# Another order of pools, conversions and evictions in a fused attention, gated MLP and mixture kernel

## The chip, the cores and the metric

One core of a Trainium2 chip runs the whole program. The time is device microseconds of one execution; where several runs are given, their median. The profile shows one further execution, taken by the hardware profiler.

## The reference

Three layers follow each other. Attention with a mask by clusters (2 batches, 8 heads, 768 positions, 64 features), a gated MLP on its 1536 tokens of 512 features, and a mixture of four experts:

```python
sims = einsum(q / |q|, centroids / |centroids|)          # the same for k; argmax over 16 clusters
scores = where(q_assign == k_assign, q @ k.T / 8, -1e9)
x = softmax(scores) @ v                                  # to 1536 x 512
x = (sigmoid(x @ w_gate) * (x @ w_val)) @ w_out          # 512 -> 1536 -> 512
p = domain_probs / (domain_probs.sum(-1) + 1e-9)
out = sum over e of p[:, e] * (relu(x @ w1[e]) @ w2[e])  # 4 experts, 512 -> 1024 -> 512
```

The weights of the MLP come as float64, everything else as float32.

## The kernel before, in words

Every fp32 product is made of three matmuls on parts of 128 x 128 by 384 or 512 columns: an operand is split into a high part (fp32r, by ScalarE, ACT) and a low part (the rest, by VectorE, DVE, or GpSimd, POOL). Within a `manual_schedule` block each engine works through its instructions in the order in which the program text issues them, so an instruction that waits holds up all that stands behind it on its engine.

**Attention.** 96 items (batch, head pair, half, 128 queries): PE makes scores S (L432), DVE their negated maximum nm (L435), ACT the exponentials (L443), PE transposes them (L452), ACT and DVE split the transposed block into ph (L455) and pl (L456), and PE multiplies with v (L465, L466). The tables SLOT, FIRST, START, EARLY, SOON and TAIL say behind which item, and where in it, each piece of other work is issued; in TAIL the items are counted from the last. `xadd` (L507) and `xscale` (L510) scale the result of a head pair and write it to X; `right_operands` makes of X the sums t1 to t4 (L525) and the operands h, l (ACT L534, DVE or POOL L537) for the MLP.

**Conversion of weights.** A float64 weight lies as two 32-bit words. "mag": ACT takes the magnitude of the high word (L653) and scales the low word (L655). "bits": DVE clips (L660), shifts (L661) and puts the sign back (L662). "round": POOL adds the low word (L667). The result is in tiles cv (w_gate, w_val) or co (w_out). Then w_gate and w_val get four sums sf (L697) and are split into w1h (ACT L705) and w1l (POOL L706); w_out is split into woh (ACT L763) and wol (POOL L764).

**Layer 1, the gated MLP** (`moe1`). The 1536 hidden features are cut into six slices p of 256, the tokens into two batches b. `gate(p, b)` and `value(p, b)` each are one `seven`: seven products of six matmuls (L788) in four PSUM banks ph, with DVE's combinations (L801 to L823) between them; the evictions of gate are ACT's sigmoid (L860), those of value DVE's product sg (L872) and its split into G (ACT L873, POOL L874). `outp(p, b)` multiplies G with w_out (48 matmuls, L672 to L674, banks po) and adds to acc (ACT L893 in p = 0, DVE L895 after). The order in the loop is gate(p,0), outp(p-1,1), value(p,0), gate(p,1), outp(p,0), value(p,1). Each call takes a list of work, issued piece by piece between its products or evictions: conversions of the next weights stand there. `outp` with `soon=True` takes four banks and first makes the f = 0 half of all four, otherwise it ends one bank after the other.

**Mixture layer** (`moe2`). 32 pairs (b, e, g); `hidden(i)` is again a `seven`, evicted by ACT as h2h (L1060) and by DVE as h2l (L1061); `outp(i)` multiplies with w2 (L1084 to L1086), DVE adds into the result (L1091). `conv_in2` makes a pair's w1h and w1l, `conv_out2` its wo parts (ACT L1040, POOL L1041) from r2, which `load_out2` (L1022) fetches into a pool of one buffer; `operands` makes the seven right operands of a batch (sums POOL L1009, splits ACT L1005, DVE or POOL L1006). The beginning of this layer's work is issued within the last calls of layer 1.

The memory of `pools` is handed on: a tile of a later pool waits until the last reader of what lay there before is done.

Of the kernel before, what the change touches and what calls it, by code (L numbers as in the profile page):

```python
# [5 lines left out]
F32 = mybir.dt.float32  # L6
# [22 lines left out]
def r2(ap):  # L29
# [50 lines left out]
class Net:  # L80
# [460 lines left out]
    def attention(self):  # L541
# [9 lines left out]
        for key in START:  # L551
            if key[0] == "W":
                self.warm(int(key[2:]))
            else:
                begin.pop(key)()
        for n in range(NP):
            steps = [(k, go) for k, go in begin.items() if k[0] == str(n)] if n < 2 else \
                [("%d %s" % (n, name), go) for name, go in self.prep(n)]
            for key, go in steps + [("%d %s" % (n, name), go) for name, go in self.finish(n)]:
                if key in FIRST:  # L560
                    at, pos = FIRST[key]
                else:
                    at, pos = SLOT[key[2:]]
                    at += n * PER
# [3 lines left out]
        def pair(o):  # L568
            pool, tags = (self.nat0, ("nk", "nq")) if o == 5 else (self.op if o in (1, 2, 6) else self.xp, ("h%d" % o, "l%d" % o))
# [6 lines left out]
        pool = self.nc.gpsimd  # L576
# [12 lines left out]
        for k in range(2):  # L589
# [8 lines left out]
                "t1": self.late[0]["t1"],  # L598
# [243 lines left out]
    def moe1(self, xadd, xscale):  # L842
# [35 lines left out]
        def outp(p, b, work=(), soon=False):  # L878
# [53 lines left out]
        for p in range(1, NP):  # L932
# [5 lines left out]
        gate(0, 0, [[lambda: split0(6, Q), vs[0]], [lambda: split0(2, V), vs[1]], [vs[2]] + d[0], d[1] + [vs[3]],  # L938
                    d[2], d[3] + d[4] + [o0["split"]], [xadd, xscale]])
# [8 lines left out]
        for p in range(1, NP):  # L948
# [24 lines left out]
        outp(NP - 1, 0, [[lambda: cin[0](Q)], [], [], [cin[1]], [cin[2]], [cin[3]], [cin[4]], [out[0]]])
# [6 lines left out]
        ys, ysplit = self.operands(0, [room(self.op, t, F32) for t in ("h1", "l1", "h2", "l2")])  # L980
# [5 lines left out]
        self.first_in = []  # L986
# [60 lines left out]
    def moe2(self):  # L1047
# [54 lines left out]
        late = self.first_in  # L1102
# [20 lines left out]
    def run(self):  # L1123
# [13 lines left out]
        with ExitStack() as a:  # L1137
# [72 lines left out]
```

## Time and profile before

| | |
|---|---|
| median of 3 runs | 1098.1 us (1096.81 to 1098.77) |
| the profiled execution | 1095.45 us, of which 1093.7 us are the span |
| mean granted clock of PE | 0.986 |
| busy, PE / DVE / POOL / ACT | 1043.5 / 821.6 / 638.9 / 549.1 us |
| chain that ended last | PE 69%, POOL 11%, DVE 8%, issue 6%, DMA 3%, ACT 2% |
| attention | until about 280 us |
| layer 1 | until about 595 us |
| mixture layer | from about 590 us to the end |

The times count from the start of the span. A busy share is a mean over stages: in the last half PE does not pause, in the first half it does. The granted clock is a fraction of PE's full rate; 0.5 is the lower of its two levels (1.2 of 2.4 GHz). In the waits, "engine line <- other line" puts an idle time of the first engine down to the instruction that released it; in the timeline the bracket behind a row is the idle time before it.

### The profile page before, as it was taken

The page shows a single profiled execution, that of the slowest core. Times are in us where ns is not written, and L with a number is a line of the kernel's source. Part 1 is how long each engine was busy: PE and PEld are TensorE (multiplying, and loading weights), DVE is VectorE, ACT ScalarE, POOL GpSimd, SP SyncE. Part 2 cuts the span into 40 slices and gives each one's busy share as a digit, 9 for nine tenths or more (in the row PEclk, how much of TensorE's full clock was granted, in tenths as well). Part 3 has the DMA queues.
Part 4 walks back from the last instruction along what each step waited for, and adds up shares of the span by engine and source line. Part 5 has one row for each costly group of instructions (what it writes and reads, how often), then busy time and mean ns, then how long its engine had stood idle before and what let it go on. Part 6 is the DMA issues. An engine that isn't in the chain of part 4 may idle for free.

```text
span 1093.7 us, 16218 instructions
## 1 busy us (share of the span) xinstructions
PE 1043.5 (95%) x5813; PEld 971.4 (89%) x5813; DVE 821.6 (75%) x1408; ACT 549.1 (50%) x1155; POOL 638.9 (58%) x567
## 2 busy tenths in 40 slices
PE   6989999998898999898999999999999999999998
PEld 6889999987698999898998999899988998999887
DVE  6979999998666676666659877776678867766765
ACT  4879999887565444444434433343334433333320
POOL 6547778776567666666778544444445644444430
PEclk8999999999999999999999999999999999999999
DMA  8677767753111111222110312221222222211201
GB/s 174 135 187 175 173 155 165 159 147 94 56 39 58 59 58 58 77 63 73 58 59 19 113 43 78 77 77 39 77 77 97 81 74 77 78 57 60 78 20 58
DMA packets 86480, 95.86 MB, mean 88 GB/s; under 512 B 42720, under 2 KB 59456, under 8 KB 86400
## 3 DMA queue, kind: packets, MB, share of 16 engines
q1 hardware_dynamic: 86256, 94.80, 31.7%
q8 instruction: 46, 0.75, 0.3%
q14 instruction: 34, 0.28, 0.1%
q10 hardware_dynamic: 144, 0.03, 0.0%
HBM read 65.07 MB, written 3.19 MB: 62 GB/s over the span
## 4 chain that ended last, share of the span: by engine, by line
PE 69%; POOL 11%; DVE 8%; issue 6%; DMA 3%; ACT 2%; SPq 0%; POOLq 0%; DVEq 0%; ACTq 0%
PE ph L788 27%; PE po L1085 8%; PE po L1086 8%; PE po L1084 8%; PE T L452 4%; PE S L432 4%; POOL w1l L706 2%; PE PV L465 2%; PE PV L466 2%; PE po L673 2%; PE po L674 1%; PE po L672 1%; DMA rwo<-in_moe_w_out_dram 1%; DMA L<-hiq 1%; POOL sf L697 1%
## 5 line engine op out<-in xcount | busy, mean ns | idle before, releaser
L1041 POOL TENSOR_TENSOR wol<-r,woh 128x512 fp32r<-128x512 f32 x62 | 80.2, 1294 | 156.9 <-ACT woh L1040 156.6
L1091 DVE SCALAR_TENSOR_TENSOR acc<-po,pn,acc 128x512 f32<-128x512 f32 (+1 forms) x181 | 129.7, 742 | 36.3 <-PE po L1086 36.3
L1086 PE MATMUL po<-woh,h2l 128*128 128x512 f32 (+1 forms) x374 | 145.7, 390 | 0.0
L1085 PE MATMUL po<-wol,h2h 128*128 128x512 f32 (+1 forms) x374 | 145.6, 389 | 0.0
L1084 PE MATMUL po<-woh,h2h 128*128 128x512 f32 (+1 forms) x374 | 145.1, 388 | 0.0
L706 POOL TENSOR_TENSOR w1l<-sf,w1h 128x512 fp32r<-128x512 f32 x88 | 115.0, 1328 | 42.7 <-ACT w1h L705 42.7
L1060 ACT ACTIVATE h2h<-ph 128x384 fp32r<-128x384 f32 x128 | 62.7, 490 | 122.4 <-PE ph L788 96.1
L788 PE MATMUL ph<-h,w1h 128*128 128x384 f32 x336 | 114.4, 341 | 5.6 <-DVE u L801 2.6
L788 PE MATMUL ph<-l,w1h 128*128 128x384 f32 x336 | 113.1, 337 | 0.9 <-POOL l L537 0.7
L788 PE MATMUL ph<-h,w1l 128*128 128x384 f32 x336 | 113.1, 337 | 0.0
L456 DVE TENSOR_TENSOR pl<-T,ph 128x384 fp32r<-128x384 f32 x192 | 97.1, 547 | 19.2 <-ACT ph L455 17.8
L705 ACT ACTIVATE w1h<-sf 128x512 fp32r<-128x512 f32 x88 | 55.4, 632 | 82.7 <-DVE sf L697 68.1
L1061 DVE SCALAR_TENSOR_TENSOR h2l<-ph,h2h 128x384 fp32r<-128x384 f32 x128 | 70.9, 554 | 34.0 <-ACT h2h L1060 30.8
L455 ACT ACTIVATE ph<-T 128x384 fp32r<-128x384 f32 x192 | 84.5, 492 | 18.0 <-PE T L452 16.9
L435 DVE TENSOR_REDUCE nm<-S 128x1 f32<-128x768 f32 x96 | 90.9, 947 | 2.0 <-PE S L432 1.1
L432 PE MATMUL S<-R,L 80*128 80x384 f32 (+1 forms) x384 | 92.1, 362 | 0.2
L452 PE MATMUL T<-ident,P 128*128 128x128 f32 x576 | 83.3, 278 | 9.4 <-DVE pl L456 8.4
L706 POOL TENSOR_TENSOR w1l<-r,w1h 128x512 fp32r<-128x512 f32 x64 | 68.6, 1074 | 38.1 <-ACT w1h L705 38.1
L443 ACT ACTIVATE P<-S,nm 128x768 f32<-128x768 f32 x96 | 87.5, 912 | 2.5 <-DVE nm L435 2.1
L452 PEld LDWEIGHTS T<-ident,P 128*128 128x128 f32 x576 | 67.7, 142 | 17.5 <-DVE pl L456 12.0
L1086 PEld LDWEIGHTS po<-woh,h2l 128*128 128x128 f32 x374 | 70.2, 188 | 14.5
L1085 PEld LDWEIGHTS po<-wol,h2h 128*128 128x128 f32 x374 | 70.2, 188 | 13.9
(276 smaller groups left out, 2860.2 us busy)
## 6 DMA issues: line engine op xcount, KB each, us to landing
r<-in_moe_w_dram SPq DMA_DIRECT2D x64, 512.0 KB, 4.5
L<-hiq SPq DMA_DIRECT2D x32, 192.0 KB, 4.8
R<-hik SPq DMA_DIRECT2D x32, 192.0 KB, 4.9
raw<-in_moe_w_val_dram SPq DMA_DIRECT2D x12, 512.0 KB, 3.8
rwo<-in_moe_w_out_dram SPq DMA_DIRECT2D x11, 512.0 KB, 3.5
raw<-in_moe_w_gate_dram SPq DMA_DIRECT2D x10, 512.0 KB, 3.6
nq<-in_q_dram SPq DMA_DIRECT2D x16, 192.0 KB, 3.8
nk<-in_k_dram SPq DMA_DIRECT2D x16, 192.0 KB, 4.4
```

Of the source, the lines that this page charges most:

```text
L432: nc.tensor.matmul(ps[:, a, 0:384], l[0:k, c], r[0:k, a * 384:a * 384 + 384], start=l is L1, stop=l is L2)
L435: nc.vector.tensor_reduce(nm, ps[:, :, 0:384], axis=AX.XY, op=ALU.max, negate=True)
L443: nc.scalar.activation(r2(pt), ps[:, :, 0:384], AF.Exp, bias=nm, scale=1.0, accum_out=P["sums"][:, i:i + 1])
L452: nc.tensor.transpose(ps[:, j, :], pt[:, c:c + 128], self.ident)
L455: nc.scalar.activation(hi, ps, AF.Copy)
L456: nc.vector.tensor_tensor(lo, ps, hi.bitcast(F32), op=ALU.subtract)
L706: nc.gpsimd.tensor_tensor(lo[:, sl], x, hi[:, sl].bitcast(F32), op=ALU.subtract)
L788: nc.tensor.matmul(ps, x[:, a, j], y[:, j], start=first and j == 0 and k == 0, stop=j == 1 and k == 2, skip_group_check=not first)
L1084: nc.tensor.matmul(ps, Hh[:, f, c], wh[:, dc], start=f == 0, stop=False)
L1085: nc.tensor.matmul(ps, Hh[:, f, c], wl[:, dc], start=False, stop=False)
L1086: nc.tensor.matmul(ps, Hl[:, f, c], wh[:, dc], start=False, stop=f == 1)
L1091: nc.vector.scalar_tensor_tensor(a, ps, pe, a, op0=ALU.mult, op1=ALU.add)
```

## The change

It has six parts.

1. *Pools* (`run`). In the attention the pools stand in the order pp, sm, ac, up, vvp, qk, ptp (qk was first). Behind it tmp, wom and a new pool opx (operands h1, l1, h2, l2, h6, l6) come ahead of co, sg and op; these six operands lay in op before.
2. *TAIL*. The three bits of each w_val half are issued in one item, the rounding right behind them in the same item; xadd and xscale of the last head pair but one come behind the second rounding, t1 at the third item from the end.
3. *SOON*. The loads, magnitudes, bits and roundings of w_gate and the first part of w_out stand at other, mostly later items; a load is further ahead of its magnitude.
4. *gate(0, 0)*. The split of o0 is issued behind the first product, the steps of o1's conversion one place later each.
5. *The loop*. The conversion e of o1 moves from value(p, 0) to gate(p, 1); its split comes behind the fifth product. outp(p, 0) has `soon=True`. In outp(0, 0) and outp(5, 1) the first half starts with two of the three matmuls of all four banks.
6. *The end of layer 1*. The sums of conv_in2(1) go from DVE to POOL; conv_out2(0) and load_out2(1) go to the end of outp(5, 1).

```diff
 TAIL = {
     "open": (-12, 0), "load10": (-12, 0), "load11": (-12, 0), "sums0": (-12, 2), "outer1": (-11, 2),
-    "split00": (-11, 2), "split01": (-11, 2), "split02": (-10, 2), "split03": (-10, 2), "t1": (-10, 2),
-    "mag10": (-9, 2), "bits10": (-8, -8, -7), "round10": (-7, 2), "mag11": (-7, 2), "bits11": (-6, -6, -5),
-    "round11": (-5, 2), "sums1": (-3, 2), "table": (-3, 2),
+    "split00": (-11, 2), "split01": (-11, 2), "split02": (-10, 2), "split03": (-10, 2),
+    "mag10": (-9, 2), "bits10": (-8, -8, -8), "round10": (-8, 1), "mag11": (-7, 2), "bits11": (-6, -6, -6),
+    "round11": (-6, 1), "xadd6": (-5, 0), "xscale6": (-5, 0), "sums1": (-5, 2), "t1": (-3, 2), "table": (-3, 2),
 }
...
-            def part(ps, d, c, f):
+            def part(ps, d, c, f, some=range(3)):
                 dc = slice(d * 128, d * 128 + 128)
                 t = self.outers[2 * p + f]
-                self.mm3(ps, t["hi"][:, dc], t["lo"][:, dc], Gh[:, f, c], Gl[:, f, c], f == 0, f == 1)
+                for k in some:
+                    x, y = (("hi", Gh), ("lo", Gh), ("hi", Gl))[k]
+                    nc.tensor.matmul(ps, t[x][:, dc], y[:, f, c], start=f == 0 and k == 0, stop=f == 1 and k == 2)
...
                 if soon:
                     banks = [bank() for _ in range(4)]
-                    for d in range(4):
-                        part(banks[d], d, c, 0)
+                    for some in ((0, 1), (2,)) if n == 0 and (p == 0 or b == 1) else (range(3),):
+                        for d in range(4):
+                            part(banks[d], d, c, 0, some)
...
-        gate(0, 0, [[lambda: split0(6, Q), vs[0]], [lambda: split0(2, V), vs[1]], [vs[2]] + d[0], d[1] + [vs[3]],
-                    d[2], d[3] + d[4] + [o0["split"]], [xadd, xscale]])
+        split0(6, Q)
+        split0(2, V)
+        gate(0, 0, [[vs[0], o0["split"]], [vs[1]] + d[0], [vs[2]] + d[1], [vs[3]] + d[2], d[3] + d[4], [], [xadd, xscale]])
...
+            value(p, 0, [[], [o0["split"]]])
             e = conv(o1)
-            value(p, 0, [[], [o0["split"]], [], e[0], e[1], e[2], e[3] + e[4]])
             if p + 1 < NP:
                 c, d, split = conv(g, 0), conv(g, 1), g["split"]
-                gate(p, 1, [[o1["split"]], c[0], c[1], c[2], c[3], c[4]])
+                gate(p, 1, [e[0], e[1], e[2], e[3] + e[4], [o1["split"]] + c[0], c[1] + c[2], c[3] + c[4]])
                 outers[2 * p + 2]["load"]()
-                outp(p, 0, [d[0], d[1], d[2], d[3] + d[4], total(g), [split[0]], [], [split[1]]])
+                outp(p, 0, [d[0], d[1], d[2], d[3] + d[4], total(g), [split[0]], [], [split[1]]], soon=True)
                 value(p, 1, [load(U[p + 1][1]), [split[2]], [split[3]]])
-        gate(NP - 1, 1, [[o1["split"]]])
+        gate(NP - 1, 1, [e[0], e[1], e[2], e[3] + e[4], [o1["split"]]])
         self.load_out2(0)
...
-        outp(NP - 1, 0, [[lambda: cin[0](Q)], [], [], [cin[1]], [cin[2]], [cin[3]], [cin[4]], [out[0]]])
+        outp(NP - 1, 0, [[lambda: cin[0](Q)], [], [], [cin[1]], [cin[2]], [cin[3]], [cin[4]], []])
...
-        value(NP - 1, 1, [[ys[0], out[1], lambda: self.load_out2(1)], [lambda: ysplit(0, V), ys[1]], [ys[2]], [], [], [],
-                          [cin[0], lambda: ysplit(4, V)]])
-        outp(NP - 1, 1, [[ys[3], lambda: ysplit(5, V)], [cin[1]], [lambda: ysplit(3, V)], [cin[2]],
-                         [lambda: ysplit(1, V)], [cin[3]], [lambda: ysplit(6, Q)], [lambda: ysplit(2, V), cin[4]]], soon=True)
+        value(NP - 1, 1, [[ys[0]], [lambda: ysplit(0, V), ys[1]], [ys[2]], [ys[3]], [], [], [lambda: ysplit(4, V)]])
+        outp(NP - 1, 1, [[lambda: ysplit(5, V), lambda: cin[0](Q)], [], [lambda: ysplit(3, V)], [cin[1]],
+                         [lambda: ysplit(1, V)], [cin[2]], [lambda: ysplit(6, Q), cin[3]],
+                         [lambda: ysplit(2, V), cin[4], out[0], out[1], lambda: self.load_out2(1)]], soon=True)
```

Of SOON one line, then the pools:

```diff
-    "load00": (12, 2), "load01": (13, 2), "abs00": (15, 2), "low00": (24, 2), "bits00": (24, 25, 27), "round00": (28, 2),
+    "load01": (13, 2), "load00": (14, 2), "abs01": (24, 2), "bits01": (25, 27, 36), "low01": (27, 2), "round01": (37, 2),
...
-            self.qk = self.pool(a, "qk", 3)
             self.pp = self.pool(a, "pp", 3)
             self.sm = self.pool(a, "sm", 2)
             self.ac = self.pool(a, "ac", 1)
+            self.up = self.pool(a, "up", 2)
             self.vvp = self.pool(a, "vvp", 2)
+            self.qk = self.pool(a, "qk", 3)
             self.ptp = self.pool(a, "ptp", 2)
-            self.up = self.pool(a, "up", 2)
...
-        self.tmp = self.pool(es, "tmp")
...
+            self.tmp = self.pool(m, "tmp")
+            self.wom = self.pool(m, "wom", 2)
+            self.opx = self.pool(m, "opx")
             self.co = self.pool(m, "co")
-            self.wom = self.pool(m, "wom", 2)
             self.sg = self.pool(m, "sg")
             self.op = self.pool(m, "op")
```

In the changed kernel the lines of the MLP carry numbers that are 4 higher up to outp, 6 or 7 higher behind it.

The change on POOL in the attention's tail, first before (tB is t1, the second and the last row with cv are the roundings of w_val, A and R are xadd and xscale, sf the sums):

```order
L525 TENSOR_TENSOR tB<-R_62 128x768
L667 TENSOR_TENSOR cv<-cv,raw 128x512
L507 TENSOR_TENSOR A<-A,W 128x768
L510 TENSOR_TENSOR R_62<-A,rb 128x768
L667 TENSOR_TENSOR cv<-cv,raw 128x512
L697 TENSOR_TENSOR sf<-cv 128x256
```

and now:

```order
L671 TENSOR_TENSOR cv<-cv,raw 128x512 x2
L507 TENSOR_TENSOR A<-A,W 128x768
L510 TENSOR_TENSOR R_62<-A,rb 128x768
L701 TENSOR_TENSOR sf<-cv 128x256
L701 TENSOR_TENSOR sf<-sf,cv 128x256
L701 TENSOR_TENSOR sf<-cv 128x256
L701 TENSOR_TENSOR sf<-cv,sf 128x256
L525 TENSOR_TENSOR tB<-R_62 128x768
```

The second rounding has moved ahead of xadd and xscale, beside the first, and tB from the front to the end, behind the sums.

DVE from value(3, 0) into gate(3, 1), before (u, ph and sg are the products' combinations and the gating; co is the conversion of o1, cv that of the next w_gate):

```order
L872 TENSOR_TENSOR sg<-sg,ph_5700 128x384
L872 TENSOR_TENSOR sg<-sg,ph_5680 128x384
L660 TENSOR_SCALAR co<-co 128x512
L818 TENSOR_TENSOR ph_5732<-u_5679,ph_5732 128x384
L661 TENSOR_SCALAR co<-co 128x512
L823 TENSOR_TENSOR ph_5708<-u_5678,ph_5708 128x384
L872 TENSOR_TENSOR sg<-sg,ph_5732 128x384
L872 TENSOR_TENSOR sg<-sg,ph_5708 128x384
L662 SCALAR_TENSOR_TENSOR co<-rwo,co 128x512
L801 TENSOR_TENSOR u_5758<-m_5757,ph_5772 128x384
```

and now:

```order
L876 TENSOR_TENSOR sg<-sg,ph_5683 128x384
L822 TENSOR_TENSOR ph_5731<-u_5682,ph_5731 128x384
L827 TENSOR_TENSOR ph_5711<-u_5681,ph_5711 128x384
L876 TENSOR_TENSOR sg<-sg,ph_5731 128x384
L876 TENSOR_TENSOR sg<-sg,ph_5711 128x384
L805 TENSOR_TENSOR u_5754<-m_5753,ph_5767 128x384
L664 TENSOR_SCALAR co<-co 128x512
L809 TENSOR_TENSOR u_5755<-u_5754,ph_5776 128x384
L665 TENSOR_SCALAR co<-co 128x512
L813 TENSOR_TENSOR ph_5776<-u_5755,ph_5785 128x384
L666 SCALAR_TENSOR_TENSOR co<-rwo,co 128x512
```

The three steps of co have left the gating products of value(3, 0) and stand between the combinations of gate(3, 1).

ACT from the last splits of layer 1 to the first evictions of the mixture layer, before (w1h is conv_in2(1), wo conv_out2(0), woh conv_out2(1), h2h the evictions of hidden(0)):

```order
L1005 ACTIVATE Y_6871<-acc_4113 128x768
L705 ACTIVATE w1h<-sf 128x512
L1005 ACTIVATE tA<-l_6875 128x768
L1005 ACTIVATE Y_6871<-acc_4113 128x768
L705 ACTIVATE w1h<-r_6547 128x256
L797 ACTIVATE A<-ph_7067 128x384
L1040 ACTIVATE woh<-r_6892 128x512
L1060 ACTIVATE h2h<-ph_7067 128x384
```

and now:

```order
L1012 ACTIVATE tA<-l_6875 128x768
L709 ACTIVATE w1h<-sf 128x512
L1012 ACTIVATE Y_6871<-acc_4116 128x768
L709 ACTIVATE w1h<-r_6550 128x256
L1047 ACTIVATE wo_7042<-r_6780 128x512
L1047 ACTIVATE wo_7045<-r_6780 128x512
L801 ACTIVATE A<-ph_7072 128x384
L1047 ACTIVATE woh<-r_7048 128x512
L1067 ACTIVATE h2h<-ph_7072 128x384
```

Both wo, which stood some ten rows further up, next to value(5, 1)'s first product, have moved behind the splits of layer 1, with only the copy of a first product between them and woh, and r_7048 comes by the transfer that load_out2(1) issues.

## Rows read from the trace of the kernel before

**Rows 1.** Waits of PE: engine, line waited for, us in total, times, longest.

```profile
PE ph L788 <- DVE sg L872: 11.3, 6, 2.2
PE T L452 <- DVE pl L456: 8.4, 6, 2.7
PE ph L788 <- DVE ph L809: 5.6, 5, 1.5
...
PE po L673 <- POOL G L874: 3.2, 2, 2.5
```

**Rows 2.** Windows: length, busy us (instructions) by engine, granted clock, DMA share, GB/s.

```profile
280.00:300.00 20.00, 15.34 (x72) 12.58 (x70) 14.13 (x19) 10.39 (x20) 15.46 (x11) 0.94 0.19 60
297.40:304.70 7.30, 6.56 (x21) 6.01 (x21) 4.62 (x7) 2.65 (x5) 5.46 (x6) 0.53 0.01 2
268.30:270.00 1.70, 1.70 (x7) 1.70 (x6) 1.57 (x4) 1.55 (x4) 1.54 (x3) 0.50 0.22 33
584.70:587.60 2.90, 2.90 (x11) 2.90 (x10) 2.90 (x2) 2.39 (x5) 2.90 (x3) 0.50 0.00 0
407.40:410.40 3.00, 3.00 (x11) 3.00 (x10) 1.08 (x2) 0.47 (x1) 2.50 (x3) 0.53 0.00 0
640.00:660.00 20.00, 20.00 (x100) 17.74 (x99) 16.17 (x29) 7.55 (x15) 8.80 (x8) 1.00 0.33 106
```

**Rows 3.** Timeline, attention: start, us, engine, instruction, idle before it and releaser.

```profile
72.62 0.66 ACT L653 ACTIVATE R<-R 128x512 f32<-128x512 f32 x1 [4.50 <-DMA R<-in_moe_w_gate_dram]
...
254.19 2.14 DVE L660 TENSOR_SCALAR cv<-cv 128x512 f32<-128x512 f32 x1
254.22 1.83 POOL L525 TENSOR_TENSOR tB<-R 128x768 f32<-128x768 f32 x1
...
258.50 0.68 DVE L662 SCALAR_TENSOR_TENSOR cv<-raw,cv 128x512 int32<-128x512 int32 x1
...
262.59 1.87 POOL L510 TENSOR_TENSOR R<-A,rb 128x768 f32<-128x768 f32 x1
...
262.83 1.91 DVE L661 TENSOR_SCALAR cv<-cv 128x512 int32<-128x512 int32 x1
...
265.26 0.55 PE L452 MATMUL T<-ident,P 128*128 128x128 f32 x3 [2.72 <-DVE pl L456]
```

**Rows 4.** Timeline, first value product of layer 1.

```profile
292.26 1.30 POOL L764 TENSOR_TENSOR wol<-R,woh 128x512 fp32r<-128x512 f32 x1
...
293.60 2.00 DVE L510 TENSOR_TENSOR R<-A,rb 128x768 f32<-128x768 f32 x1 [2.46 <-POOL wol L764]
...
296.12 0.45 PE L788 MATMUL ph<-h,w1h 128*128 128x384 f32 x1 [2.59 <-DVE u L801]
```

**Rows 5.** Timeline, value(4,0) and gate(4,1).

```profile
503.36 0.67 ACT L653 ACTIVATE co<-rwo 128x512 f32<-128x512 f32 x1 [0.88 <-DMA rwo<-in_moe_w_out_dram]
...
504.06 0.43 DVE L660 TENSOR_SCALAR co<-co 128x512 f32<-128x512 f32 x1 [1.68 <-ACT co L653]
...
506.27 0.45 PE L788 MATMUL ph<-g,w1h 128*128 128x384 f32 x1 [1.99 <-DVE sg L872]
...
511.63 1.06 DVE L660 TENSOR_SCALAR cv<-cv 128x512 f32<-128x512 f32 x1 [2.40 <-ACT cv L653]
```

**Rows 6.** Timeline, end of layer 1; last, POOL's group of L697 (busy, mean ns).

```profile
580.81 4.45 POOL L874 TENSOR_TENSOR G<-sg,G 128x384 fp32r<-128x384 f32 x4
...
594.94 1.45 POOL L706 TENSOR_TENSOR w1l<-r,w1h 128x256 fp32r<-128x256 f32 x1
...
599.48 1.28 POOL L1041 TENSOR_TENSOR wol<-r,woh 128x512 fp32r<-128x512 f32 x1 [1.84 <-ACT woh L1040]
...
602.09 0.44 PE L788 MATMUL ph<-h,w1h 128*128 128x384 f32 x1
...
604.89 0.63 ACT L1040 ACTIVATE woh<-r 128x512 fp32r<-128x512 f32 x1 [2.35 <-DMA r<-in_moe_w_dram]
...
L697 POOL TENSOR_TENSOR sf<-cv 128x256 f32<-128x256 f32 x22 | 16.3, 741 | 0.9
```

More of the change, by code (lines that the diff above doesn't have):

```diff
@@ L66 @@
 SOON = {
-    "load00": (12, 2), "load01": (13, 2), "abs00": (15, 2), "low00": (24, 2), "bits00": (24, 25, 27), "round00": (28, 2),
-    "abs01": (27, 2), "low01": (36, 2), "bits01": (36, 37, 39), "round01": (40, 2),
-    "loado": (29, 2), "abso": (39, 2), "lowo": (48, 2), "bitso": (48, 49, 51), "roundo": (52, 2),
+    "load01": (13, 2), "load00": (14, 2), "abs01": (24, 2), "bits01": (25, 27, 36), "low01": (27, 2), "round01": (37, 2),
+    "abs00": (36, 2), "bits00": (37, 39, 48), "low00": (39, 2), "round00": (49, 2),
+    "loado": (50, 2), "abso": (56, 2), "bitso": (57, 60, 61), "lowo": (60, 2), "roundo": (62, 2),
 }
@@ L555, in attention @@
                 begin.pop(key)()
+        scale6 = {}
         for n in range(NP):
@@ L561, in attention @@
                     at, pos = FIRST[key]
+                elif key in ("%d xadd" % (NP - 2), "%d xscale" % (NP - 2)):
+                    scale6[key[2:] + "6"] = go
+                    continue
                 else:
@@ L568, in pair @@
         def pair(o):
-            pool, tags = (self.nat0, ("nk", "nq")) if o == 5 else (self.op if o in (1, 2, 6) else self.xp, ("h%d" % o, "l%d" % o))
+            pool, tags = (self.nat0, ("nk", "nq")) if o == 5 else (self.opx if o in (1, 2, 6) else self.xp, ("h%d" % o, "l%d" % o))
             return [pool.tile([128, 2, HB], F32R, name=t, tag=t) for t in tags]
@@ L597, in attention @@
         tail = {"open": self.open_weights, "outer1": lambda: self.outers[1]["load"](),
-                "t1": self.late[0]["t1"],
+                "t1": self.late[0]["t1"], **scale6,
                 "table": lambda: self.nc.scalar.activation(self.warm1, self.half[:, 0:1], AF.Sigmoid)}
@@ L979, in moe1 @@
         self.Y = Y
-        ys, ysplit = self.operands(0, [room(self.op, t, F32) for t in ("h1", "l1", "h2", "l2")])
+        ys, ysplit = self.operands(0, [room(self.opx, t, F32) for t in ("h1", "l1", "h2", "l2")])
         cin = self.conv_in2(1)
-        value(NP - 1, 1, [[ys[0], out[1], lambda: self.load_out2(1)], [lambda: ysplit(0, V), ys[1]], [ys[2]], [], [], [],
-                          [cin[0], lambda: ysplit(4, V)]])
-        outp(NP - 1, 1, [[ys[3], lambda: ysplit(5, V)], [cin[1]], [lambda: ysplit(3, V)], [cin[2]],
-                         [lambda: ysplit(1, V)], [cin[3]], [lambda: ysplit(6, Q)], [lambda: ysplit(2, V), cin[4]]], soon=True)
-        self.first_in = []
+        value(NP - 1, 1, [[ys[0]], [lambda: ysplit(0, V), ys[1]], [ys[2]], [ys[3]], [], [], [lambda: ysplit(4, V)]])
+        outp(NP - 1, 1, [[lambda: ysplit(5, V), lambda: cin[0](Q)], [], [lambda: ysplit(3, V)], [cin[1]],
+                         [lambda: ysplit(1, V)], [cin[2]], [lambda: ysplit(6, Q), cin[3]],
+                         [lambda: ysplit(2, V), cin[4], out[0], out[1], lambda: self.load_out2(1)]], soon=True)
     def open_mixture(self):
@@ L1101, in moe2 @@
         sums, split = self.operands(1, [self.block(0, k, n) for k in range(2) for n in range(2)])
-        late = self.first_in
+        late = []
         for i in range(LAST):
```

## The prediction

> **What bounds the kernel now.** I read the windows of the late kernel first, to see where nothing can be won. From 640 us on PE is busy for 20.00 us of each 20 at the full granted clock [rows 2]: the mixture layer is bound by PE's own work, and the change touches none of its instructions. All that can be gained lies where PE waits before it, or runs at the lower of its two rates because it had waited.
>
> PE's waits come next [rows 1]: 11.3 us for DVE's gating product sg (six times), 8.4 us for DVE's pl in the attention, 5.6 us for DVE's ph sum L809, and 3.2 us for POOL's G, of which one wait is 2.5. Three of the four lead to DVE. The timeline then says why DVE is late, and it is not the same everywhere. In the attention's tail it is DVE's own instruction that is long: L660 takes 2.14 us beside POOL's tB, and L661 1.91 us beside POOL's L510, where an L660 with nothing beside it takes 0.43 [rows 3, 5]. Between the layers DVE's L510 starts late, because POOL's L764 reads the rows that it overwrites [rows 4]. In the loop DVE stands still in front of a conversion step until ACT's L653 has its data, and the gating products are queued behind it [rows 5].
>
> Last, the windows of the lower clock: 7.3 us at 0.53 after the stall at 296, 1.7 us at 0.50 after that at 265, 3.0 us at 0.53 in the loop, 2.9 us at 0.50 near the end [rows 2]. Each follows a wait of some 2 us or more; a stretch of length s at 0.5 costs s/2.
>
> **The change, part by part.** The sum is made against the profiled execution, 1095.45 us; the median of the runs, 1098.1, lies 2.65 above, and I add that at the end.
>
> *Attention's tail (TAIL table).* The bits now run while POOL waits for them, and xadd6, xscale6 and tB come behind both roundings. Two L660 and one L661 fall from 2.14, about 1.9 and 1.91 us to about 0.43: DVE gets back 1.7 + 1.5 + 1.5 = 4.7 us. The third step, L662 of 0.68 us [rows 3], now stands ahead of pl in the same item, so I take back 0.6: 4.1 us. The two waits that these clashes make (2.72 [rows 3], and a smaller one before it) hold about that much of the 8.4. With the slow stretch of 1.7 us at 0.50 (0.85 us): **-5.0**. Ends: 0, if POOL's later work meets other DVE instructions instead, and -9.3, all of pl's waits and the stretch. POOL is past three instructions more when it reaches tB; tB's first reader is far behind, so that is covered.
>
> *From attention to the first half of layer 1 (pools, gate(0,0)).* The operands h1, l1, h2, l2, h6, l6 now lie where q and k lay, and can be written before the last PV products have read their inputs; o0's wol is taken out of X at the first step, so L510 has not to wait 2.46 us for it, and PE not 2.59 for L801 [rows 4]. PE is idle for 20.00 - 15.34 = 4.66 us of 280 to 300, waits 3.2 - 2.5 = 0.7 for the first G, and loses 7.3 x 0.47 = 3.4 at the low clock [rows 1, 2]: 8.8 us. Since the chains begin earlier too, by the time PE now loses refilling after five waits, I take **-9.3**. Ends: -3 (only L510's wait goes) and -10.
>
> *The loop.* o1's conversion moves from value(p,0), where five sg waits depend on it, into gate(p,1). A longest wait is 2.2 us; by the timeline these five are 9.8 of the row's 11.3 us [rows 1] (the sixth, at 330, is elsewhere and stays), and three waits for ph L809, behind a cv step that ran 1.06 us and waited 2.40 [rows 5], are 4.4 of that row's 5.6. That is 14.2 us; the refill of PE adds about 0.15 at each of eight, 1.2, and two slow stretches of 3.0 us at 0.53 add 2.8 [rows 2]: 18.2. Against it: a remnant of 0.2 to 0.3 at each of five seams, 1.2; and outp(p,0) now holds all four banks at once, so that DVE's eviction has half the slack that it had: four times 0.4, estimated 1.8 with the conversion step in front. **-15.2**. Ends: -18.2, and -7 if every gate(p,1) keeps a wait like the old L809 one (five times 1.5) and outp(p,0) gets some too.
>
> Here a rule of the Trainium skill speaks against the change (SBUF - State Buffer, "Who interferes with whom"): VectorE and GpSimd lock one pair of ports for a whole instruction, whichever issues first. The tail's 2.14 against 0.43 us agrees. In gate(p,1) the moved steps meet POOL's G and wol; by the rule it is then DVE that is late again, which is the first rival below.
>
> *The end of the layer.* conv_out2(0) goes behind everything else of outp(5,1), and load_out2(1), which uses the same single buffer, waits for its second wo on POOL. Before, POOL ended its four G at 585.26 and the last w1l at 596.39: 11.1 us in a row [rows 6]. Now one l (about 2.0) is ahead of the last three G, four sums of 0.74 come in [rows 6], and two wo of 1.28 (as wol is): POOL is done at about 585.8 + 9.1 + 3.0 + 2.6 = 600.5 with the durations of before, and at 597.8 if the w1l, no longer beside DVE's sums, run as short as wol. I take 599.3. The DMA then needs what it needed from 600.76 to ACT's start at 604.89, 4.13 us [rows 6]; woh takes 0.63, to 604.1. Behind this woh on ACT stand all four evictions of hidden(0), and PE can start the second product of hidden(1) only when three of them and the second woh are through, 4 ACT instructions of at most 0.63 and their DVE halves: about 2.7, 606.8, where it was 602.09 [rows 6]. That is +4.7; a wait of 4 us should bring a slow stretch like that of 2.9 us at 0.50, while the one after the G wait stays, since G's second piece is no earlier than its first reader: +0.8 between none and 1.5. **+5.5**, ends +3 and +9. The new order of outp(5,1) and outp(0,0) only lets eight products run before a late G is needed: some 0.6 us, hidden by the wait that follows.
>
> *Early conversions (SOON table).* ACT's wait of 4.50 us at 72.62 [rows 3] goes, as the magnitude comes 12 items after its load. But the chain there goes on through a transfer that the change does not move, so I take nothing for it, and +0.5 for conversion steps that now fall beside other work. Ends -4.5 and +2.
>
> **Sum:** -5.0 - 9.3 - 15.2 + 5.5 + 0.5 = -23.5. The profiled execution would be 1071.95; with 2.65, the forecast is **1074.5**.
>
> **Rivals.**
> *A, DVE is blocked at the new place.* For it: L660 ran 1.06 us beside POOL's wol in just this gate [rows 5]. Against it: a gate has four banks, and DVE has some 1 us of slack per product. Five gates at the old wait of 1.6 make +8: 1082.5. Also 1082 to 1084 is what comes out if the transition keeps its waits because something else still holds the new buffers (the change then does not do what it says there). Together 0.20, of which the second 0.05.
>
> *B, slower.* load_out2 has one buffer, and each load waits for POOL's wol of the load before. If the lateness at the end does not die out but is passed on, every pair of the mixture layer starts late. One round is DMA 4.13 + woh 0.63 + an eviction + woh 0.63 + wol 1.28, about 7.5 us, and PE needs about 15 us for a pair (32 pairs in the 490 us after 602 us, PE full throughout). So a pair catches up 7 us, and the lateness should be gone in one. It decides from a round longer than a pair's 15 us: say a queue makes it 16, then 30 pairs at 1 us give +30: 1104.5. Chance 0.04.
>
> *C, more is gained.* ACT's 4.50 us at 72.62 were on the path after all, or the last wait is covered: 1066 to 1069. Against it: PE's chain at that place goes over the transfer. Chance 0.14.
>
> **How the numbers follow.** The forecast (1070 to 1080) has 0.62, A 0.20, C 0.14, B 0.04. The likeliest case gives the time, 1074.5. The range goes from 1066.0, which takes in most of C, to 1086.0, which takes in A: about 1 in 10 is left out above, with B, and 1 in 20 below. A difference of 0.2% (2.2 us) is about what a measurement of this kernel can tell from no change: all cases but B are faster by more. Faster 0.95, same 0.01, slower 0.04.
>
> **What would show it.** Right: no L660 or L661 over 1 us in the attention's tail, and the waits for pl there under 4 us in all; no wait for u L801 near 290; waits for sg L872 under 3 us in all; a new wait of PE of 3 to 6 us about 27 to 30 us after the start of value(5,1), with woh waiting for r2's DMA in front of it; full windows in the mixture layer from some 20 us later. Wrong: waits for ph L809 or for a po bank of 1.5 us in each p (A); PE idle in the mixture layer between pairs (B); the end's wait missing (C). If the tail's items are as long as before, the clash was not what made them long.

## The result, and the profile after

The changed kernel takes 1086.4 us (median of 4 runs, 1084.3 to 1088.5) against 1097.5 of before on the same chip: a ratio of 0.990, 95% interval 0.9874 to 0.9926, 11 us faster. The forecast was 1074.5, with 1066 to 1086: the direction was right, the gain less than half as large. The profiled execution took 1087.25 us, 0.9 above this median, where that of before lay 2.0 below its own; so the traces show 8.2 us of the 11. One later execution, the profiled one of e6_w_later, was disturbed (1145.8 us, a granted clock of 0.847) and is neither read nor counted.

Some waits of PE in the changed kernel (engine, line waited for, us in total, times, longest):

```profile
PE PV L465 <- ACT U L472: 11.8, 6, 6.8
PE ph L792 <- DVE h2l L1068: 6.4, 1, 6.4
...
PE po L891 <- ACT acc L899: 3.0, 3, 1.7
...
PE T L452 <- DVE pl L456: 2.4, 6, 0.7
PE po L891 <- POOL G L878: 1.8, 2, 1.5
PE po L891 <- DVE acc L901: 1.7, 4, 0.4
...
PE ph L792 <- DVE sg L876: 1.5, 1, 1.5
```

Against [rows 1] the removed waits are gone as forecast: sg from 11.3 to 1.5 us, pl from 8.4 to 2.4, ph L813 (L809 of before) from 5.6 to nothing. Not all of pl's was the tail's: one wait of 2.46 us at 74.31 stood behind ACT's wait for its weight [rows 3] and went with that, so the tail's end of -9.3 took in too much. The new wait for h2l is there too. What nobody had priced is the first line: 11.8 us for U, in the attention.

To see where the time went, the same instruction is compared in both traces: the n-th maximum of the attention (DVE L435, counted from 0) and the first eviction of a `seven` (ACT L797, in the changed kernel L801). The table gives its start less its start in the kernel before, in us, also for the versions run later. Each row is one execution; kernels with the same attention differ there by up to 4.5 us (e9_splits and e10_sums_pool at max 56).

| | max 18 | max 23 | max 56 | max 65 | max 90 | max 95 | gate(0,1) | value(5,1) | hidden(3) |
|---|---|---|---|---|---|---|---|---|---|
| before, start | 68.8 | 86.3 | 168.6 | 190.1 | 253.3 | 270.0 | 313.3 | 574.1 | 633.4 |
| changed | -0.6 | +3.7 | +3.9 | +9.5 | +7.4 | +2.8 | -3.1 | -14.8 | -8.2 |
| e1_soon_old | -1.2 | -0.7 | -1.0 | -0.2 | -0.8 | -5.4 | -12.5 | -24.3 | -17.5 |
| e2_end_old | -0.6 | +0.3 | -0.2 | +6.3 | +4.2 | -0.5 | -6.3 | -17.8 | -17.2 |
| e3_soon_alone | -1.1 | +1.8 | +2.1 | +7.7 | +5.5 | +5.6 | +5.5 | +5.0 | +5.0 |
| e4_both_old | -0.8 | -0.1 | +1.6 | +1.2 | +1.9 | -2.7 | -8.5 | -20.2 | -19.5 |
| e5_o_later | -0.4 | +1.3 | +1.7 | +2.0 | +3.2 | -1.5 | -8.5 | -20.4 | -14.4 |
| e7_banks | -0.9 | +1.6 | +2.4 | +9.4 | +7.5 | +2.9 | -4.1 | -15.2 | -9.5 |
| e8_both_new | -1.3 | -6.1 | -4.6 | -4.0 | -3.2 | -7.8 | -14.9 | -26.9 | -26.2 |
| e9_splits | -1.1 | -6.0 | -5.2 | -4.7 | -2.8 | -7.5 | -15.9 | -26.8 | -26.2 |
| e10_sums_pool | +1.5 | -2.4 | -0.7 | -0.7 | +0.6 | -4.0 | -9.9 | -21.5 | -20.4 |
| e11_no_loop | -0.9 | -0.6 | +0.5 | +0.2 | 0.0 | -4.6 | -11.7 | -11.1 | -11.1 |

In the changed kernel the attention up to the tail loses 8.0 us (max 18 to max 90), the tail gives 4.6 back, the seam to gate(0,1) 5.8, the loop up to value(5,1) 11.7; the end of the layer loses 6.6. The rest of the mixture layer adds nothing: hidden(3) is as late as the end of the span.

**The attention.** The timeline of the changed kernel around its two new waits (start, us, engine, instruction, idle before it):

```profile
67.06 1.23 SPq L723 DMA_DIRECT2D R<-in_moe_w_gate_dram  x2
...
69.97 1.27 SPq L395 DMA_DIRECT2D R<-hik  x2
...
80.80 0.49 ACT L266 ACTIVATE hik<-T 128x384 fp32r<-128x384 f32 x1 [6.97 <-DMA R<-hik]
...
81.72 0.69 PE L465 MATMUL PV<-ph,vv 128*128 128x384 f32 x1 [6.76 <-ACT U L472]
...
165.57 0.67 SPq L751 DMA_DIRECT2D R<-in_moe_w_out_dram  x1
...
167.90 1.24 SPq L395 DMA_DIRECT2D R<-hik  x2
...
176.13 0.49 ACT L266 ACTIVATE hik<-T 128x384 fp32r<-128x384 f32 x1 [2.92 <-DMA R<-hik]
...
184.00 4.49 POOL L227 TENSOR_TENSOR sq<-sq 128x768 f32<-128x768 f32 x5
...
185.04 1.09 DVE L664 TENSOR_SCALAR R<-R 128x512 f32<-128x512 f32 x1
```

ACT writes hik (L266) only when the DMA has copied the last head's rows out of it (R<-hik, L395). Just ahead of those copies weight loads of 512 KB are issued, two at 67.06 and one at 165.57; ACT waits 6.97 and 2.92 us, and U, and PE behind U, wait with it. In the kernel before, ACT stood 4.50 us for its own weight first [rows 3], PE waited 2.46 us behind that, and L266 waited 1.87 us more:

```profile
74.31 1.01 PE L452 MATMUL T<-ident,P 128*128 128x128 f32 x6 [2.46 <-DVE pl L456]
...
79.27 0.49 ACT L266 ACTIVATE hik<-T 128x384 fp32r<-128x384 f32 x1 [1.87 <-DMA L<-hiq]
```

Behind PE's long wait the clock falls too. These are the windows after it, first before, then changed:

```profile
75.70:79.10 3.40, 3.40 (x16) 3.21 (x15) 3.15 (x6) 1.69 (x4) 1.01 (x1) 0.50 1.05 235
...
80.00:86.80 6.80, 5.08 (x21) 4.47 (x22) 3.00 (x5) 5.01 (x10) 4.20 (x4) 0.50 0.13 30
```

The last two rows of the changed kernel's timeline are a second, smaller loss: the first of w_out's bits, now at item 57, runs beside POOL's L227, and L664 takes 1.09 us instead of 0.43.

**The tail** went as said. The bits stand ahead of POOL's roundings, and each step has its short time, where [rows 3] had 2.14 and 1.91:

```profile
266.69 0.42 DVE L664 TENSOR_SCALAR cv<-cv 128x512 f32<-128x512 f32 x1
...
267.15 0.43 DVE L665 TENSOR_SCALAR cv<-cv 128x512 int32<-128x512 int32 x1
...
267.61 0.69 DVE L666 SCALAR_TENSOR_TENSOR cv<-raw,cv 128x512 int32<-128x512 int32 x1
```

**The seam** to layer 1 lost its waits for u [rows 4], but has another in outp(0,0):

```profile
299.72 5.06 POOL L525 TENSOR_TENSOR cv<-tA,R 128x768 f32<-128x768 f32 x2
...
302.31 0.84 ACT L534 ACTIVATE g<-cv 128x768 fp32r<-128x768 f32 x1 [1.33 <-POOL cv L525]
...
303.06 0.47 ACT L899 ACTIVATE acc<-po 128x384 f32<-128x384 f32 x1
...
303.58 0.45 PE L891 MATMUL po<-G,woh 128*128 128x384 f32 x1 [1.69 <-ACT acc L899]
```

ACT stands 1.33 us for POOL's sum of operand 5, the eviction of acc behind it, and PE 1.69 us for a free bank. The window after it ran at a granted clock of 0.66:

```profile
304.00:309.00 5.00, 4.68 (x19) 4.35 (x18) 3.35 (x4) 3.82 (x8) 1.93 (x2) 0.66 0.00 0
```

**The end** is the chain of the forecast, link by link:

```profile
582.93 2.50 POOL L1048 TENSOR_TENSOR wo<-r,wo 128x512 fp32r<-128x512 f32 x2
585.46 7.18 SPq L1029 DMA_DIRECT2D r<-in_moe_w_dram  x2
...
589.03 0.63 ACT L1047 ACTIVATE woh<-r 128x512 fp32r<-128x512 f32 x1 [10.61 <-DMA r<-in_moe_w_dram]
589.57 0.47 ACT L1067 ACTIVATE h2h<-ph 128x384 fp32r<-128x384 f32 x1
...
590.68 0.69 PE L792 MATMUL ph<-h,w1h 128*128 128x384 f32 x1 [6.38 <-DVE h2l L1068]
```

POOL ends the second wo at 585.43, the load is issued, woh starts 3.6 us later, h2h and h2l follow, and PE has waited 6.38 us. From 591 on the clock is 0.56 for 5 us.

### The profile page after: what moved, and what is told of

It is laid out like the page before. It is cut to its first block, busy times and chain, and to the rows that moved or that the text cites. A ratio compares the mean times of both kernels' runs of the same rounds, so it can differ in the third digit from the quotient of the medians.

```text
span 1085.4 us, 16225 instructions
## 1 busy us (share of the span) xinstructions
PE 1039.6 (96%) x5813; PEld 966.2 (89%) x5813; DVE 821.5 (76%) x1404; ACT 547.9 (50%) x1155; POOL 639.0 (59%) x571
## 4 chain that ended last, share of the span: by engine, by line
PE 62%; DVE 5%; POOL 3%; issue 2%; ACT 1%; DMA 0%; POOLq 0%; DVEq 0%; ACTq 0%
PE ph L792 32%; PE po L1093 8%; PE po L1092 8%; PE po L1091 8%; PE po L891 6%; DVE cv L664 1%; DVE ph L827 1%; POOL co L671 1%; POOL G L878 1%; DVE sg L876 1%; DVE acc L901 1%; POOL sf L701 0%; POOL w1l L710 0%; DVE ph L813 0%; DVE u L805 0%
## 5 line engine op out<-in xcount | busy, mean ns | idle before, releaser
L891 PE MATMUL po<-G,woh 128*128 128x384 f32 x384 | 105.4, 343 | 6.5 <-ACT acc L899 3.0
L435 DVE TENSOR_REDUCE nm<-S 128x1 f32<-128x768 f32 x96 | 91.1, 949 | 2.0 <-PE S L432 1.3
L455 ACT ACTIVATE ph<-T 128x384 fp32r<-128x384 f32 x192 | 84.4, 493 | 14.9 <-PE T L452 13.9
```

Source lines behind the costliest of these rows:

```text
L435: nc.vector.tensor_reduce(nm, ps[:, :, 0:384], axis=AX.XY, op=ALU.max, negate=True)
L455: nc.scalar.activation(hi, ps, AF.Copy)
L891: nc.tensor.matmul(ps, t[x][:, dc], y[:, f, c], start=f == 0 and k == 0, stop=f == 1 and k == 2)
```

## The experiments

Each kernel is compared by its ratio to the kernel before on its own chip (1097.3, 1094.4 and 1095.9 us in the three groups); a step of 0.001 is 1.1 us. The ratios are those on record with their intervals; the quotient of the two medians differs from them by up to 0.0012.

**1. The early table undone** (e1_soon_old). The lines of SOON as before, everything else of the change kept:

```diff
-    "load01": (13, 2), "load00": (14, 2), "abs01": (24, 2), "bits01": (25, 27, 36), "low01": (27, 2), "round01": (37, 2),
+    "load00": (12, 2), "load01": (13, 2), "abs00": (15, 2), "low00": (24, 2), "bits00": (24, 25, 27), "round00": (28, 2),
...
-    "loado": (50, 2), "abso": (56, 2), "bitso": (57, 60, 61), "lowo": (60, 2), "roundo": (62, 2),
+    "loado": (29, 2), "abso": (39, 2), "lowo": (48, 2), "bitso": (48, 49, 51), "roundo": (52, 2),
```

> The changed kernel with the SOON table of before. Theory 1 (the new places of the early conversions cost the attention 8.0 us in the trace, since 512 KB weight loads now stand right ahead of the transfers of the q and k rows that ACT's L266 waits for): some 7.5 us under the changed kernel, about 1079 us, with item 23 of the attention as early as in the kernel before. Theory 2 (the delay is made up later anyway, or was the DMA's luck in one profile): within 2 us of the changed kernel, 1085 to 1088 us.

Measured: 1080.2 us, 0.9835 of before (0.9804 to 0.9865), some 7 us under the changed kernel's 0.990. In the table max 65 is at -0.2 in place of +9.5, and nothing is made up later: hidden(3) is 9.3 earlier (1.2 of that are a slow stretch in the seam that this trace lacks). Theory 1's size holds. That the loads make it this run does not show, since it undoes the whole table.

**2. The end undone** (e2_end_old): `conv_out2(0)`, `load_out2(1)` and the sums of `conv_in2(1)` at their places of before.

```diff
-        outp(NP - 1, 0, [[lambda: cin[0](Q)], [], [], [cin[1]], [cin[2]], [cin[3]], [cin[4]], []])
+        outp(NP - 1, 0, [[lambda: cin[0](Q)], [], [], [cin[1]], [cin[2]], [cin[3]], [cin[4]], [out[0]]])
...
-        value(NP - 1, 1, [[ys[0]], [lambda: ysplit(0, V), ys[1]], [ys[2]], [ys[3]], [], [], [lambda: ysplit(4, V)]])
+        value(NP - 1, 1, [[ys[0], out[1], lambda: self.load_out2(1)], [lambda: ysplit(0, V), ys[1]], [ys[2]], [], [], [],
+                          [cin[0], lambda: ysplit(4, V)]])
```

> The changed kernel with the end of layer 1 as before (sums of conv_in2(1) on DVE, conv_out2(0) and load_out2(1) at their old places). Theory 1 (load_out2(1) waits for the late wo, and the evictions of hidden(0) for its woh): the wait of 6.4 us for h2l goes, 5 to 6.5 us under the changed kernel, 1080 to 1081.5 us. Theory 2 (POOL's chain of G, l and w1l is what PE waits for there, wherever wo stands): the wait shrinks by 2 us at most, 1084.5 us or more.

Measured: 1078.9 us, 0.9826 (0.9799 to 0.9853), 8 us under the changed kernel, a little more than expected. The wait for h2l is gone; from value(5,1) to hidden(3) the table now loses 0.6 us, not 6.6. In its place PE waits 2.0 us once for acc (L901), behind DVE's l. Theory 1 holds.

**3. The early table alone**, on the kernel before (e3_soon_alone); the diff is that of experiment 1, turned round.

> The kernel before with the new SOON table alone. Theory 1: 7 to 8 us slower than before, about 1105 us, all of it between items 18 and 66 of the attention. Theory 2: within 2 us of before, 1095.5 to 1099.5 us.

Measured: 1101.3 us, 1.0038 (1.0019 to 1.0058): slower by 2 to 6 us, and in neither theory's range. Its trace loses 2.9 us from max 18 to 23 and 5.6 from 56 to 65, gets 2.1 of it back by max 90, and is 5.0 us late at the end. The loss is at the places of experiment 1, its size smaller; the first of the two places differs from profile to profile (4.3 us in the changed kernel, 2.9 here, 2.5 in e7_banks, 0.9 in e2_end_old), the second less (5.6, 5.6, 7.0, 6.5).

**4. Both undone** (e4_both_old).

> The changed kernel with both the SOON table and the end of before. If the two losses are independent (theory 1): 12 to 14 us under the changed kernel, 1072.5 to 1074.5 us. If one hides behind the other or both are made up later (theory 2): 1079 us or more.

Measured: 1075.3 us, 0.9788 (0.9757 to 0.9819), 12 us under the changed kernel, a little short of the 15 that the two alone give, and nearer to theory 1 than to theory 2. The table ends at -19.5. The three parts that are left, forecast at -29.5 together, are worth 20 us by the trace and 22 to 23 by the times.

**5. Only w_out's early load moved** (e5_o_later).

```diff
-    "loado": (50, 2), "abso": (56, 2), "bitso": (57, 60, 61), "lowo": (60, 2), "roundo": (62, 2),
+    "loado": (53, 2), "abso": (56, 2), "bitso": (57, 60, 61), "lowo": (60, 2), "roundo": (62, 2),
```

> The changed kernel with the load of w_out's first part at item 53 in place of 50, behind the transfers of the q and k rows of item 52. Theory 1 (a 512 KB load right ahead of these transfers makes them late for ACT's L266): the attention loses nothing at item 57, where the changed kernel's trace loses 3.0 us, and the time is 2 to 4 us less, 1082.5 to 1084.5 us. Theory 2 (the later conversion steps beside POOL's work lose it, the load does not): item 57 as late as in the changed kernel, time within 1 us of it.

Measured: 1081.8 us, 0.9884 (0.9851 to 0.9917), against 0.990: by the time alone unclear. By the trace it is decided. The copies now stand ahead of the load, and L266 waits for nothing:

```profile
165.06 1.18 SPq L395 DMA_DIRECT2D R<-hik  x2
...
169.65 0.83 SPq L751 DMA_DIRECT2D R<-in_moe_w_out_dram  x1
...
170.74 0.52 ACT L266 ACTIVATE hik<-T 128x384 fp32r<-128x384 f32 x1
```

From max 56 to 65 it loses 0.4 us where the changed kernel lost 5.6. But a later stretch, up to max 70, loses 2.1 here and nothing there, so that from max 56 to 90 it is 1.5 against 3.5 us (3.4 to 5.1 in the other three traces with the load at item 50): the load's place makes at least 2 us of the second half of the loss, as theory 1 has it. What makes the rest is open; e4_both_old, with the old table, also loses 1.5 us from max 65 to 70. The conversion steps beside POOL, which stayed, lose 0.7 us (max 57 to 60).

**6. Only w_gate's loads moved** (e6_w_later).

```diff
-    "load01": (13, 2), "load00": (14, 2), "abs01": (24, 2), "bits01": (25, 27, 36), "low01": (27, 2), "round01": (37, 2),
+    "load01": (17, 2), "load00": (18, 2), "abs01": (24, 2), "bits01": (25, 27, 36), "low01": (27, 2), "round01": (37, 2),
```

> The changed kernel with the two loads of w_gate at items 17 and 18 in place of 13 and 14, behind the row transfers of item 16. Theory 1: L266's wait of 7.0 us at item 20 shrinks to under 1 us, items 19 to 23, which lose 4.4 us against before in the changed kernel, lose under 0.5, and the time is 3 to 5 us less, 1081.5 to 1083.5 us. Theory 2 (L266 waits for its own row transfers, whatever stands before them): L266 waits 3 us or more, and the time is within 1 us of the changed kernel.

Measured: 1079.0 us (three runs), 0.9856 (0.9823 to 0.9890), some 5 us under the changed kernel's ratio, as theory 1 has it. The steps between items are read from experiment 8, which has the same loads.

**7. One bank after the other in outp(p, 0)** (e7_banks): `soon=True` taken out of that call in the loop.

> The changed kernel with outp(p, 0) ending one bank after the other, as before the change (p = 1 to 4); o1's conversion stays in gate(p, 1). Theory 1 (four banks at once cost a wait for acc and short ones beside it, 1.2 us in each of four in the trace): these go, but the first low part of o1 is then needed 1 us earlier; 1 to 4 us less, 1082.5 to 1085.5 us. Theory 2 (without four banks PE waits for o1's wol in each outp): four waits of 1 to 2 us for POOL's wol, 2 to 6 us more than the changed kernel.

Measured: 1085.3 us, 0.9911 (0.9880 to 0.9941): no difference. Neither theory came out as a whole. The waits for acc went, and in their place PE waits in five outp for POOL's wol, 0.9 us each:

```profile
PE po L891 <- POOL wol L768: 4.6, 5, 0.9
```

The old order costs what the four banks cost: the moved conversion is ready just too late for it.

**8. New places for the whole table, old end** (e8_both_new): experiments 2, 5 and 6 together, and w_out's bits, low words and rounding put where they had stood in the period of 12 items.

```diff
-    "load01": (13, 2), "load00": (14, 2), "abs01": (24, 2), "bits01": (25, 27, 36), "low01": (27, 2), "round01": (37, 2),
+    "load01": (17, 2), "load00": (18, 2), "abs01": (24, 2), "bits01": (25, 27, 36), "low01": (27, 2), "round01": (37, 2),
-    "loado": (50, 2), "abso": (56, 2), "bitso": (57, 60, 61), "lowo": (60, 2), "roundo": (62, 2),
+    "loado": (53, 2), "abso": (58, 2), "bitso": (60, 61, 63), "lowo": (60, 2), "roundo": (64, 2),
```

> The changed kernel with the end of before, both w_gate loads at 17 and 18, w_out's load at 53, its magnitude at 58, its bits at 60, 61 and 63 (the places in the period of 12 that they had before) and its rounding at 64. Theory 1 (loads ahead of row transfers, and bits beside POOL's work, are the whole loss of the new table): 4 to 6 us under the changed kernel with the end of before alone (1078.85), 1073 to 1075 us, and no later at item 70 than the kernel before. Theory 2 (it is the later conversion itself): 1077.5 us or more.

Measured: 1071.3 us, 0.9783 (0.9754 to 0.9812), 5 us under e2_end_old by ratio. From max 18 to 23 it is not only free of the loss but 4.8 us ahead of the kernel before, which had waited there for its own loads; PE's clock does not fall there. From max 56 to 90 it loses 1.4 us, as much as experiment 5, so the better place of the bits shows in items 57 to 60 alone (0.0 in place of 0.7). The first copies stand ahead of the loads here too:

```profile
67.39 1.19 SPq L395 DMA_DIRECT2D R<-hik  x2
...
72.39 1.93 SPq L723 DMA_DIRECT2D R<-in_moe_w_gate_dram  x2
...
73.21 0.49 ACT L266 ACTIVATE hik<-T 128x384 fp32r<-128x384 f32 x1
```

**9. The splits of outp(0, 0) in another order** (e9_splits), on top of experiment 8:

```diff
-        outp(0, 0, [[lambda: split(4, V)], [lambda: split(5, V)], [lambda: split(3, V)], [lambda: split(1, V)],
+        outp(0, 0, [[lambda: split(4, V)], [lambda: split(3, V)], [lambda: split(1, V)], [lambda: split(5, V)],
```

> The version of the last call that was fastest (end of before, new places for the early conversions, 0.978 of before) with the splits in outp(0, 0) in the order 4, 3, 1, 5, so that ACT does not stand in front of POOL's late sum for operand 5 with the eviction of acc behind it. Theory 1 (that wait is what the changed order put in the place of the removed ones between attention and layer 1): PE's waits for acc there, 1.65 and 0.33 us, go or halve, and gate(0, 1) starts 1 to 3 us earlier; 0.975 to 0.977 of before. Theory 2 (POOL's chain of G and sums sets the end of outp(0, 0) anyway, so the wait only moves into gate(0, 1)): within 0.5 us of it, 0.978.

Measured: 1070.0 us, 0.9768 (0.9745 to 0.9790): the fastest version of the study, though its interval overlaps that of experiment 8. PE's longest wait for acc falls from 1.65 to 1.01 us (the one left is in outp(0,1)), and gate(0,1) stands at -15.9 instead of -14.9. But gate(0,1) then waits 0.64 us for the low part of operand 5, which takes DVE 2.60 us beside POOL's W, and one `seven` later both versions are level (-14.9). So the wait moves on, as in theory 2, though behind DVE as much as behind POOL:

```profile
295.75 2.25 POOL L537 TENSOR_TENSOR W<-cv,A 128x768 fp32r<-128x768 f32 x1 [1.15 <-ACT A L534]
...
296.21 2.60 DVE L537 TENSOR_TENSOR k<-cv,g 128x768 fp32r<-128x768 f32 x1
...
298.87 0.44 PE L792 MATMUL ph<-k,w1h 128*128 128x384 f32 x1 [0.64 <-DVE k L537]
```

**10. The sums of conv_in2(1) on POOL** (e10_sums_pool): as experiment 8, but of the end only `out[0]`, `out[1]` and `load_out2(1)` at their old places.

> That same fastest version, but with the sums of conv_in2(1) on POOL and in the changed kernel's places; only conv_out2(0) and load_out2(1) stand as before. Theory 1 (the late load is the whole of the loss at the end, the sums on POOL are harmless): PE's wait of 2 us for acc behind DVE's l (L1014) goes and no wait over 2 us comes for h2l; within 1.5 us of that version either way, 0.977 to 0.9795 of before. Theory 2 (POOL, with four sums of 0.74 us more, delivers w1l of pair 1 late): a wait of 3 us or more at the start of hidden(1), 0.981 or more.

Measured: 1070.4 us, 0.9779 (0.9749 to 0.9809), as fast as experiment 8. No wait for h2l comes, so the late load was the loss, and the sums of conv_in2(1) cost nothing that the time shows. But PE waits 3.6 us once for G, behind POOL's wo and the mixture layer's operand sums (L1016), instead of 1.3 for G and 2.0 for acc.

**11. Without the loop** (e11_no_loop): TAIL, pools, gate(0, 0) and the order of matmuls alone; SOON, the loop and the end as before.

> The kernel before with only the TAIL table, the pools, gate(0, 0) and the order of matmuls in outp(0, 0) and outp(5, 1) of the changed one (loop, SOON and end as before). Theory 1 (the tail gives 4 to 5 us and the seam to layer 1 about 6, independent of the loop): 9 to 11 us under before, 0.990 to 0.992 of it, so that the loop's part, against the version with the old SOON and end (0.979), is 11 to 13 us. Theory 2 (the loop would have absorbed the earlier start, or the gain of the loop hangs on it): 0.995 or more.

Measured: 1085.6 us, 0.9909 (0.9887 to 0.9930), as expected. Tail and seam are worth 11.7 us in its trace and stay through the rest; the old waits of the loop are back:

```profile
PE ph L792 <- DVE sg L876: 12.0, 6, 2.8
...
PE ph L792 <- DVE ph L813: 4.6, 4, 1.5
```

Against experiment 4 (0.9788) the loop is worth 0.012, 13 us.

## Why the prediction was wrong

It was wrong in one term above all: the early conversions, which make 7.5 of the 15.3 us that the trace misses. Seam and loop, with the mechanism right and the size too large, make 3.5 each. Without the loss of the early table (experiment 1) the ratio of 0.9835 makes 1079.4 us, inside the range. Forecast and measured, in the changed kernel's trace:

| term | forecast | trace |
|---|---|---|
| early conversions (SOON) | +0.5, ends -4.5 and +2 | +8.0 |
| attention's tail | -5.0 | -4.6 |
| seam to layer 1 | -9.3 | -5.8 |
| loop | -15.2 | -11.7 |
| end of the layer | +5.5 | +6.6 |
| start of the attention | 0 | -0.6 |

**Early conversions: the step that failed.** The text saw ACT's wait of 4.50 us at 72.62 [rows 3] and that "the chain there goes on through a transfer that the change does not move", and took nothing for it. The transfer did not move, but what stands ahead of it on SP's queue did matter: w_out's load was moved from behind the copies of its period to right ahead of them, and the text never asked where a moved load lands in the queue, although each DMA of a moved step was there to be counted. Experiments 1 and 3 show the loss (7 and 4 us by the times; the 8.0 are one trace), 5 that the place of a single load makes at least 2 of the 3.5 us of its second half, 6 and 8 the same for the two loads of the first half. An upper end of +2 was too low where ACT's 4.50 us in [rows 3] were already a wait for such loads. Whether the copies are late because they stand behind the load on SP's queue, or because the load takes up the same DMA engines, is not separated: no run issues it from another queue.

For w_gate's loads the order on the queue is the same before and after, and part of the loss was there before: PE's 2.46 us at 74.31 and the slow stretch behind it. So the premise of rival C was right, and experiment 8, 4.8 us ahead of the kernel before, has what it hoped for. In the changed kernel, with ACT's wait gone, the attention ran 4 us ahead (max 19 and 20) and then stood at L266 instead. L266 itself starts at 78.2 to 79.3 us in the four other traces with the loads at items 13 and 14, no later than with the old table (78.6 to 79.3); in the changed kernel's it starts at 80.80, and why is open. A further part is the price of one long wait: the stretch at 0.50 behind it lasts 6.8 us where it lasted 3.4 before, 1.7 us more. It lasts 6.8 in e3_soon_alone and e7_banks also, 3.4 in e2_end_old and e5_o_later, and those two lose least there (0.9 and 1.7 us).

**DVE beside POOL** had been set against the loop (rival A). There it cost little: L664 of the moved conversion takes 0.91 to 0.93 us beside POOL's G in gate(p, 1), in place of 0.43, its L665 keeps 0.41 to 0.42, and PE does not wait for them; its waits are one of 0.4 us for acc in each outp(p, 0), and some short ones. It did show in the early conversions, where the text had not looked: L664 at 1.09 us beside POOL's L227, with 0.7 us lost at these items in experiment 5, though by max 90 experiment 8, which is free of it, is no further ahead.

**The seam.** The waits of [rows 4] went as argued. Taken as if nothing were late next, the term missed that POOL's two sums of 2.5 us each follow the G of value(0,0) directly, and that ACT's split of operand 5 stands for them ahead of the evictions. Experiment 9 shows that without this wait PE meets the next one, for the same operand, 0.64 us long. In the changed kernel the stretch at 0.66 came on top; in experiments 8 and 11, whose waits are the same, it did not, and the seam gave 7.1 us.

**The loop.** All eight waits are gone, as forecast. The five for sg were sized right: from value(p, 0) to gate(p, 1) the five slices gain 9.5 us, and 9.8 with the refill and less the remnants is 9.4. The other part was mis-sized: three waits for L809 (4.4 us) and two slow stretches (2.8) were to go at a new cost of 1.8 in outp(p, 0), 5.9 us net with the refill. This is the time from the first eviction of gate(p, 1) to that of value(p, 1), with PE's waits in it, in us:

| | p = 1 | 2 | 3 | 4 | 5 |
|---|---|---|---|---|---|
| before | 16.87 | 16.86 | 16.89 | 16.87 | 16.69 |
| of it waits | 1.48 | 0 | 1.50 | 1.45 | 0 |
| changed | 16.45 | 16.45 | 16.50 | 16.45 | 16.48 |
| of it waits | 0.42 | 0.42 | 0.42 | 0.42 | 0.91 |

Before, p = 2 and 5 had 3.4 us at the lower clock in place of the wait. Waits and slow stretches are gone, but all five together gain only 1.9 us here and 0.6 right behind: the new cost is larger. A stretch of as many products without a wait takes 15.1 us (gate(p, 0) to value(p, 0)), so each outp(p, 0) costs some 1.2 us, 0.42 of it the wait for acc, where the forecast had 0.4; in outp(5, 0) PE waits 0.91 us for wol. Experiment 7 shows that the old order would cost as much.

**The end** was right in mechanism and size: PE waited 6.38 us, the forecast had some 5 and a slow stretch. Experiments 2 and 10 show that the late load makes it. Rival B is excluded: ACT waits for r's transfer three times (16.9 us in all), pair 2 loses a last 0.8 us, and the mixture layer is even from there on.

The terms add up as stated; with 2.65 the sum is 1074.6, and w_gate's first magnitude comes 11 items after its load (13 to 24), not 12, which changes nothing. The sum was made against a profiled execution and moved to the median by 2.65 us; for the changed kernel the two lie the other way round, so that 2.9 us of the miss in the trace is not one in the medians.

## What to carry to other kernels

When a step that begins with a transfer is moved, write down what stands behind it on its DMA queue and who waits for that: here one 512 KB load just ahead of six copies of 192 KB made their reader wait 2.92 us. A wait that goes is only a gain up to the next wait on the same engine, so follow the chain of the next late item before booking it. In a loop of a fixed period, moving a step by anything but whole periods can put it beside other work, as w_out's bits beside L227.

## What was not expected of the hardware

The same load of 512 KB, issued ahead of the row copies, made L266 wait 2.92 us, and issued 4.6 us behind the first of them (e5_o_later) made it wait for nothing. The same wait of PE of 1.7 us in outp(0,0) was followed by a clock of 0.66 over 5 us in the changed kernel and in experiments 2, 4 and 10, and in experiments 1, 5, 7, 8 and 11 the window behind it ran at full clock. In experiment 8:

```profile
293.00:299.00 6.00, 5.67 (x31) 5.36 (x32) 4.83 (x4) 5.31 (x11) 3.04 (x2) 1.00 0.00 0
```

The seam gave 5.8 to 5.9 us in the four and 7.0 to 7.1 in the five, so some 1.2 us hang on it. What tells the two apart is open.
